# A windowed attention with a two-layer network on one core: the first batch's loads in two parts, shorter mask work on GpSimd, and a newly planned order

## The chip, the cores and the metric

The kernel runs on one core of one Trainium2 chip. The metric is the time of one execution in device microseconds (us). One profiled execution of the kernel before lies beside three timed runs of it.

## What is computed

The reference has two stages. A causal attention with a window of 64 runs over 8 batches, 8 heads, 576 tokens and a head dimension of 64; its result, laid out as 4608 tokens of 512 channels, goes through two matrix products with x * sigmoid(x) between them.

```python
scores = np.matmul(q, k.transpose(0, 1, 3, 2)) / np.sqrt(64)
mask = (rel >= 0) & (rel < 64)
attn = softmax(np.where(mask, scores, -1e9))
x = np.matmul(attn, v).transpose(0, 2, 1, 3).reshape(4608, 512)
h = x @ w_in                       # 512 x 2048
out = (h * (1.0 / (1.0 + np.exp(-h)))) @ w_out   # 2048 x 512
```

All five inputs lie in memory as 32-bit numbers; the loads turn them into 16-bit ones (bf16). The output is 32-bit.

## The kernel before

**Order.** Nothing is scheduled while the kernel is built. Every piece of work (a load, one transposition, the scores of some blocks, one product) is put into a list by `Plan.add` (L38), and `Plan.run` (L43) emits the pieces in the order of one long string, `ORDER` (L55): a word such as `93P2` says piece 93, on PE, into PSUM bank 2. Each engine then works through its own queue in that order, and waits where its next instruction lacks an operand or a free buffer. There are 1643 words. The costs and priorities given to `add` play no part at run time.

**Tiles.** The tokens are cut into 9 tiles of 512. Tile t needs the attention of 8 blocks of 64 tokens, for two "quads" of 4 heads each. One such piece of attention is a visit: scores on PE (L292), exponentials on ScalarE (`expo`, L307), a mask on VectorE (`masking`, L314), values on PE (L323), a reciprocal and a product on VectorE (L334, L338), and the transposition of the result into the tile's `xt` (`turn_out`, L442).

**Tile 0** is done plainly. Its attention comes in visits of four blocks, and the mask is added by four more matmuls per visit (L285, with `ident` and `block`). `first_plain` (L450) multiplies w_in with half a tile's 256 tokens, two feature tiles at a time and over four channel groups; quad 0 gives channel groups 0 and 1, quad 1 gives 2 and 3. For the first 256 tokens and the first four pairs the product is split in two pieces, so that the half with quad 0's channels can go first (`SPLIT` in the loop that makes the pieces). `silu_plain` (L461) writes the activations into `gall`, a ring of 10 slots for all tiles, and `second_plain` (L464) multiplies them with w_out.

**Tiles 1 to 8** go through a scheme with 7 products in place of 8: sums of tokens (`xsum`, L485 and L487) and of weights (`wsum1`, `wsum2`, L469) before the products (L507), copies ("forks", L523, on ScalarE or VectorE) and additions ("joins", L526, on VectorE) after them, the activation L529 into `gall`, sums of activations (`gsum`, L493 and L496), and the second layer's seven products (L519) with forks and joins again. The output of a tile is stored by SP (L533).

**Loads** are all issued by GpSimd (POOL) in the order of `ORDER`. Batch 0's and 1's q and k come as one transfer per quad and tensor (`load_quad`, L224: 128 partitions with 18 tokens each, 1152 numbers per partition), later batches head by head (L227). A quad's q or k is transposed by VectorE (`turn_quad`, L255 and L258, for batches 0 and 1; `turn_blocks`, L265 and L268, later) into `kT` and `qT`. The buffers `nat` alternate between even and odd batches, so a load waits until the batch two before it has been transposed. v is loaded in groups of 128 tokens (L235, with L233 and L239 to L241 for the rest) and copied to the other half of the partitions (L273, L275). Weights come in eight transfers each (L245, L248).

**Constants.** POOL fills `strip` and `ident` with ones and cuts each with two `affine_select` instructions (L184 to L187, L191 to L193). While the first loads are under way PE runs products of a zero tile ("fills", L895), 36 in all.

The names in the lists of instructions below: `nat_87` and `nat_86` are k and q of quad 0 for even batches, `nat_89` and `nat_88` those of quad 1; `nat_90` to `nat_93` serve the odd batches; `vv_98` and `vv_99` hold v of the even and odd batches.

## Time and profile before

| | us |
|---|---|
| median of 3 runs | 276.85 (275.15 to 277.24) |
| span of the profiled execution | 275.0 |
| PE, DVE, ACT, POOL busy in it | 264.7, 214.0, 195.6, 129.7 |
| last store landed, end of the span | 275.0 |

The page gives no other time for the profiled execution than its span, from the first to the last instruction. The median of the runs lies 1.8 above that span, so it holds some time around it or a slower execution. The clock that the throttle granted to PE was 1.000 over the whole span. The rows of the profile give a start and a duration in us, the engine, the line, the output and inputs with their shapes, and in brackets how long the engine had been idle and what ended that.

### The profile page before, as it was taken

The numbers are of one execution on the slowest core, as the hardware profiler recorded it, in microseconds if no ns is written. First come the engines' busy times: TensorE is split into PE (matmuls) and PEld (weight loads), VectorE is DVE, ScalarE is ACT, GpSimd is POOL, SyncE is SP. The second block draws the span as 40 slices with busy tenths as digits, with TensorE's granted clock in tenths as the row PEclk, the third lists the DMA queues.
The fourth block names the chain that finished last, engine by engine and source line by source line (L and its number), as shares of the span: only waits on it lengthen the run. The fifth ranks groups of instructions, "written<-read, shape, count | busy, mean of one in ns | idle before, by whom it ended". The sixth has DMA issues, their size and how long they took to land.

```text
span 275.0 us, 10018 instructions
## 1 busy us (share of the span) xinstructions
PE 264.7 (96%) x4335; PEld 218.0 (79%) x4342; DVE 214.0 (78%) x426; ACT 195.6 (71%) x361; POOL 129.7 (47%) x194
## 2 busy tenths in 40 slices
PE   7978999999999999999999999999999999999993
PEld 2557844688888888888888888888888888888882
DVE  3757578999996898889799999988867967824741
ACT  1555993699749993987499958893888489537910
POOL 7944566988959758596387335940000000000000
PEclk9999999999999999999999999999999999999999
DMA  6999999999999959999979998990400040003004
GB/s 106 167 190 210 198 191 172 144 198 157 118 151 209 127 56 97 242 122 87 93 179 159 83 126 122 136 121 2 155 0 2 6 155 0 2 29 127 0 2 157
DMA packets 101631, 31.62 MB, mean 115 GB/s; under 512 B 92368, under 2 KB 95440, under 8 KB 101584
## 3 DMA queue, kind: packets, MB, share of 16 engines
q0 software_dynamic: 96128, 21.51, 86.1%
q1 hardware_dynamic: 5456, 9.44, 9.7%
q8 instruction: 35, 0.57, 0.9%
q14 instruction: 12, 0.10, 0.1%
HBM read 42.99 MB, written 9.44 MB: 191 GB/s over the span
## 4 chain that ended last, share of the span: by engine, by line
PE 88%; ACT 4%; DVE 4%; issue 1%; ACTq 0%
PE room L519 36%; PE room L507 35%; PE room L292 4%; PE room L323 4%; PE room L450 4%; PE room L895 4%; PE room L464 2%; ACT es L307 2%; DVE o L338 1%; ACT L307 1%; ACT g L461 1%; DVE es L314 1%; DVE xt L442 1%; PE room L285 1%; ACT L461 0%
## 5 line engine op out<-in xcount | busy, mean ns | idle before, releaser
L529 ACT ACTIVATE g<-room 128x512 bf16<-128x512 f32 x96 | 53.6, 605 | 4.5 <-PE room L507 4.1
L507 PEld LDWEIGHTS <-wsum 128*128 128x128 bf16 x512 | 49.9, 98 | 7.2 <-issue 1.0
L519 PEld LDWEIGHTS <-gsum 128*128 128x128 bf16 x512 | 49.1, 98 | 6.2 <-DVE gsum L496 0.2
L507 PE MATMUL room<-xsum,wsum 128*128 128x256 bf16 x384 | 53.3, 272 | 0.5 <-ACT es L307 0.3
L307 ACT ACTIVATE es<-room 128x512 bf16<-128x512 f32 (+1 forms) x88 | 39.1, 533 | 14.2 <-PE room L292 9.6
L519 PE MATMUL room<-wsum,gsum 128*128 128x256 bf16 x384 | 48.4, 273 | 0.0
L507 PEld LDWEIGHTS <-w_in_sb 128*128 128x128 bf16 x384 | 37.2, 98 | 4.7
L519 PEld LDWEIGHTS <-g 128*128 128x128 bf16 x384 | 36.7, 98 | 4.6
L526 DVE TENSOR_TENSOR room<-room,part 128x512 f32<-128x512 f32 (+1 forms) x41 | 27.8, 684 | 13.7 <-ACT part L523 3.5
L227 POOL DMA_DIRECT2D nat<-in_k_dram x48 | 30.0, 631 | 15.1 <-DVE kT L265 11.4
L507 PE MATMUL room<-xt,w_in_sb 128*128 128x256 bf16 x256 | 36.8, 273 | 0.0
L519 PE MATMUL room<-w_out_sb,g 128*128 128x256 bf16 x256 | 35.7, 273 | 0.0
L227 POOL DMA_DIRECT2D nat<-in_q_dram x48 | 29.9, 637 | 9.7 <-DVE qT L268 6.1
L523 ACT COPY ot<-room 128x512 f32<-128x512 f32 (+1 forms) x23 | 13.3, 582 | 28.6 <-PE room L519 21.5
L235 POOL DMA_DIRECT2D vv<-in_v_dram x32 | 29.6, 940 | 5.0 <-DMA nat<-in_k_dram 1.7
L523 ACT COPY room<-room 128x512 f32<-128x512 f32 x40 | 23.3, 592 | 12.1 <-PE room L507 10.8
L526 DVE TENSOR_TENSOR fin<-room,part 128x512 f32<-128x512 f32 x32 | 21.6, 683 | 9.0 <-PE room L507 6.1
L523 ACT COPY part<-room 128x512 f32<-128x512 f32 x40 | 23.6, 598 | 6.4 <-PE room L519 3.2
L241 POOL DMA_DIRECT2D vv<-in_v_dram x24 | 22.3, 934 | 12.0 <-PE room L323 11.5
L314 DVE TENSOR_TENSOR es<-es,strip 128x1024 bf16<-128x1024 bf16 (+1 forms) x36 | 21.9, 626 | 6.7 <-ACT es L307 6.4
L338 DVE TENSOR_TENSOR o<-room,recips 128x896 bf16<-128x896 f32 (+2 forms) x36 | 25.9, 726 | 0.8
L496 DVE TENSOR_TENSOR gsum<-g,gsum 128x512 bf16<-128x512 bf16 x64 | 25.1, 415 | 0.4
(75 smaller groups left out, 376.8 us busy)
## 6 DMA issues: line engine op xcount, KB each, us to landing
out_dram<-ot SPq DMA_DIRECT2D x16, 512.0 KB, 3.9
vv<-in_v_dram POOLq DMA_DIRECT2D x56, 128.0 KB, 5.0
nat<-in_k_dram POOLq DMA_DIRECT2D x48, 72.0 KB, 4.0
nat<-in_q_dram POOLq DMA_DIRECT2D x48, 72.0 KB, 3.7
w_in_sb<-in_moe_w_in_dram POOLq DMA_DIRECT2D x8, 256.0 KB, 9.2
w_out_sb<-in_moe_w_out_dram POOLq DMA_DIRECT2D x8, 256.0 KB, 9.0
nat<-in_k_dram POOLq DMA_DIRECT2D x4, 288.0 KB, 8.0
nat<-in_q_dram POOLq DMA_DIRECT2D x4, 288.0 KB, 8.2
```

The costliest lines, as they stand in the source:

```text
L227: queue[e].dma_start(out=nats[b % 2][a][kk][32 * h:32 * h + 32].rearrange("p (n x) -> p n x", n=NB), in_=(q, k)[kk][b, 4 * a + h].rearrang ...
L235: queue[e].dma_start(out=vv[b % 2][:, :, 2 * g + 1, 0:D], in_=v[b, :, 128 * g:128 * g + 128].rearrange("h p d -> p h d"))
L241: queue[e].dma_start(out=vv[b % 2][:, :, 2 * g, 0:D], in_=v[b, :, 128 * g - 64:128 * g + 64].rearrange("h p d -> p h d"))
L307: nc.scalar.activation(out=es_part(a, blocks)[:, h], in_=banks[bank.idx][:, 0:64 * n], func=ACTF.Exp, scale=scale)
L314: nc.vector.tensor_mul(t, t, strip[:, s:s + n].rearrange("k n i -> k (n i)").unsqueeze(1).to_broadcast([128, 2, 64 * n]))
L338: nc.vector.tensor_mul(out, at_values(bank, n)[:, :, :, 0:D], recips[:, w:w + 2 * n].rearrange("k (t n) -> k t n", t=bank.wide).unsqueeze( ...
L496: nc.vector.tensor_sub(out=dst[2 * i - 1], in0=g(1, 2 - i), in1=dst[i - 1])
L507: nc.tensor.matmul(banks[bank.idx][:, 256 * i:256 * i + 256], lhsT=lhs(z, i), rhs=rhs(z), start=(start and i == 0 and z == 0), stop=(z == ...
L519: nc.tensor.matmul(banks[bank.idx][:, 256 * m:256 * m + 256], lhsT=lhs(m, i), rhs=rhs(i), start=(start and i == 0 and m == 0), stop=(stop ...
L523: copies[e](out=dst, in_=src)
L526: nc.vector.tensor_add(out=dst, in0=bank, in1=part)
L529: nc.scalar.activation(out=g_tile(pair, 256 * t, 256 * t + 256), in_=src.rearrange("k (f t) -> k f t", f=2), func=ACTF.Silu)
```

## The change

Seven edits go together.

1. q and k of batch 0 are loaded in two parts each, tokens 0 to 255 and 256 to 575 of a quad (128 KB and 160 KB as written, in place of 288 KB), and each part is transposed by an instruction of its own. There are eight loads and eight transpositions in place of four and four. `LOADS`, which makes the loads, lists first parts (`a`), two groups of v (`u`), second parts (`b`) and the other groups; the order of issue is that of `ORDER`.
2. POOL no longer fills `strip` and `ident`: VectorE does (`const_fills`), with zeros for `ident`, whose diagonal one `affine_select` with `not_equal` sets. POOL has three mask instructions in place of six.
3. Tile 0's activations go to `g_first`, a second view of `gsum`, in place of slots of `gall`. Tile 1's activations find the ring free; tile 1's activation sums must wait for tile 0's second layer.
4. All first-layer products of tile 0 are split by channel groups, not only the first four pairs of the first half. Tile 0's `xt` is laid out by halves (`by_half`).
5. The copies of the first two groups of batch 0's v may be made by ScalarE as well.
6. The last tile's stores may be issued by ScalarE's queue as well as by SP's.
7. `ORDER` is new throughout (1664 words). Of the 36 fills 15 stand ahead of the first scores, 24 before; the first scores are quad 1's. In the last tile ScalarE issues two of the five stores. Over the whole program VectorE makes 11 of the output copies in place of 5 (rows `COPY ot`), and ScalarE loads its function tables 16 times in place of 18.

```diff
 ORDER = (
-    "1D 9G 2D 74P7 3D 11G 69P2 72P5 13G 67P0 15G 68P1 73P6 5G 70P3 71P4 19G 7D 78P3 81P6 82P7 86P3 6G 10D 77P2 89P6 90P7 75P0 17G 76P1 80P5 12D 83P0 79P4 "
+    "1D 14G 5D 4D 2D 3D 83P4 16G 76P1 89P1 91P6 30G 110P7 80P5 93P4 10G 6G 28G 12G 82P1 96P1 15D 102P4 8D 7G 19G 17D 31D 18G 107P6 92P7 11D 95P6 105P1 "
...
-        nc.gpsimd.memset(strip[:, 0], 1.0)
...
     def const_ident(_):
-        nc.gpsimd.memset(ident, 1.0)
-        nc.gpsimd.affine_select(out=ident, in_=ident, compare_op=ALU.is_ge, fill=0.0, base=0, channel_multiplier=1, pattern=[[-1, 128]])
-        nc.gpsimd.affine_select(out=ident, in_=ident, compare_op=ALU.is_ge, fill=0.0, base=0, channel_multiplier=-1, pattern=[[1, 128]])
+        nc.gpsimd.affine_select(out=ident, in_=ident, compare_op=ALU.not_equal, fill=1.0, base=0, channel_multiplier=1, pattern=[[-1, 128]])
+
+    def const_fills(_):
+        nc.vector.memset(strip[:, 0], 1.0)
+        nc.vector.memset(ident, 0.0)
...
+    PARTS = ((0, 256), (256, 576))
+
+    def load_part(e, b, a, kk, i):
+        lo, hi = PARTS[i]
+        queue[e].dma_start(out=nats[b % 2][a][kk][:, 2 * lo:2 * hi], in_=(q, k)[kk][b, 4 * a:4 * a + 4, lo:hi].rearrange("h (p c) d -> h p (c d)", p=32))
...
+    def turn_part(b, a, kk, i):
+        lo, hi = PARTS[i]
+        c = (hi - lo) // 32
+        src = nats[b % 2][a][kk][:, 2 * lo:2 * hi].bitcast(FP32)
...
+            nc.vector.transpose(out=dst.rearrange("x (p c) -> x c p", c=c), in_=src.rearrange("x (c w) -> x c w", c=c))
...
+    g_first = gsum.rearrange("k u n f t -> k (u n f t)").rearrange("k (g f t) -> k g f t", g=8, f=2)
...
-            nc.scalar.activation(out=g_tile(pr, lo, hi), in_=src[:, i], func=ACTF.Silu)
+            nc.scalar.activation(out=g_first[:, pr, :, lo:hi], in_=src[:, i], func=ACTF.Silu)
...
-        nc.tensor.matmul(banks[bank.idx], lhsT=gall[:, pair, f % 2, 128 * m:128 * m + 128], rhs=w_out_sb[:, f],
+        nc.tensor.matmul(banks[bank.idx], lhsT=g_first[:, pair, f % 2, 128 * m:128 * m + 128], rhs=w_out_sb[:, f],
...
-    LOADS = "p0-2 u0-4 i0-2 i2-4 i4-6 r0-1 i6-8 o0-2 v0-1 o2-3 r1-2 o3-4 v1-2 u4-5 o4-5 v2-4 o5-8 v4-5"
+    LOADS = "a0-2 u0-2 b0-2 u2-4 i0-2 i2-4 i4-6 r0-1 i6-8 o0-2 v0-1 o2-3 r1-2 o3-4 v1-2 u4-5 o4-5 v2-4 o5-8 v4-5"
...
+                half = [x for nb in range(lo // 64, hi // 64) for x in xt_done[nb][:1]] + [win[ft // 2][0] for ft in fts]
...
-            st = p.add({"SP": 0.45}, lambda e, i=i, r0=r0, r1=r1, lo=lo, hi=hi: store(e, j, 2 * i + r0, 2 * i + r1, lo, hi), deps, 0,
+            st = p.add({"SP": 0.45, "ACT": 0.4} if last else {"SP": 0.45}, lambda e, i=i, r0=r0, r1=r1, lo=lo, hi=hi: store(e, j, 2 * i + r0, 2 * i + r1, lo, hi), deps, 0,
```

The new order is shown at three places. The first is the start of POOL's queue, which issues every load. Before:

```order
L224 DMA nat_87<-in_k_dram 128x1152
L224 DMA nat_86<-in_q_dram 128x1152
L224 DMA nat_89<-in_k_dram 128x1152
L224 DMA nat_88<-in_q_dram 128x1152
L184 MEMSET strip 128x64
L185 ISA
L185 AFFINE_SELECT strip<-strip 128x64
L187 AFFINE_SELECT strip<-strip 128x64
L235 DMA vv_98<-in_v_dram 128x8x64
L191 MEMSET ident 128x128
L192 AFFINE_SELECT ident<-ident 128x128
L193 AFFINE_SELECT ident<-ident 128x128
```

After:

```order
L233 DMA nat_89<-in_k_dram 128x1x512
L233 DMA nat_88<-in_q_dram 128x1x512
L233 DMA nat_88<-in_q_dram 128x1x640
L233 DMA nat_87<-in_k_dram 128x1x512
L185 ISA
L185 AFFINE_SELECT strip<-strip 128x64
L187 AFFINE_SELECT strip<-strip 128x64
L233 DMA nat_89<-in_k_dram 128x1x640
L233 DMA nat_86<-in_q_dram 128x1x512
L191 AFFINE_SELECT ident<-ident 128x128
L244 DMA vv_98<-in_v_dram 128x8x64 x2
L233 DMA nat_86<-in_q_dram 128x1x640
```

Eight part loads stand where four quad loads stood. The second parts are those of 640 numbers per partition. One of them comes ahead of the strip's masks and three behind, and two groups of v stand ahead of the last two (the last row here is the first of those).

VectorE's queue at the same place, where it transposes q and k of batch 0 (L255 and L258 before, L276 and L279 after). Before:

```order
L255 STREAM_TRANSPOSE kT_96<-nat_87 128x18x32
L258 STREAM_TRANSPOSE qT_94<-nat_86 128x9x64
L255 STREAM_TRANSPOSE kT_97<-nat_89 128x18x32
L258 STREAM_TRANSPOSE qT_95<-nat_88 128x9x64
L273 COPY vv_98<-vv_98 64x8x64
L205 MEMSET vv_99 128x72
L206 MEMSET vv_99 64x8x32
L275 COPY vv_98<-vv_98 64x8x64
```

After:

```order
L276 STREAM_TRANSPOSE kT_97<-nat_89 128x8x32
L199 TENSOR_SCALAR block<-strip 128x512
L200 MEMSET block 64x64
L279 STREAM_TRANSPOSE qT_95<-nat_88 128x4x2x32
L279 STREAM_TRANSPOSE qT_95<-nat_88 128x5x2x32
L276 STREAM_TRANSPOSE kT_96<-nat_87 128x8x32
L276 STREAM_TRANSPOSE kT_97<-nat_89 128x10x32
L279 STREAM_TRANSPOSE qT_94<-nat_86 128x4x2x32
L294 COPY vv_98<-vv_98 64x8x64
L296 COPY vv_98<-vv_98 64x8x64
L279 STREAM_TRANSPOSE qT_94<-nat_86 128x5x2x32
L276 STREAM_TRANSPOSE kT_96<-nat_87 128x10x32
```

The queue now begins with quad 1's k. First parts have 8 groups of 32 for k and 4 by 2 for q, second parts 10 and 5 by 2. The second parts of quad 0 (`nat_86`, `nat_87`) stand behind the first two copies of v.

The second place is VectorE's queue at the beginning of tile 1, from the sums of tokens (`xsum`) to the first joins (`room<-room,part`). Before:

```order
L485 TENSOR_TENSOR xsum<-xt_76 128x2x512
L487 TENSOR_TENSOR xsum<-xt_76,xsum 128x512
L469 TENSOR_TENSOR wsum_72<-w_out_sb 128x512 x2
L487 TENSOR_TENSOR xsum<-xt_76,xsum 128x512
L265 STREAM_TRANSPOSE kT_96<-nat_87 128x9x2x32
L526 TENSOR_TENSOR room<-room,part_79 128x512
L469 TENSOR_TENSOR wsum_72<-wsum_72,w_out_sb 128x512
L526 TENSOR_TENSOR room<-room,part_80 128x512
L526 TENSOR_TENSOR fin_81<-room,part_79 128x512
```

After:

```order
L511 TENSOR_TENSOR xsum<-xt_76 128x2x512
L513 TENSOR_TENSOR xsum<-xt_76,xsum 128x512 x2
L495 TENSOR_TENSOR wsum_72<-w_out_sb 128x512 x2
L495 TENSOR_TENSOR wsum_72<-wsum_72,w_out_sb 128x512
L495 TENSOR_TENSOR wsum_72<-w_out_sb 128x512
L495 TENSOR_TENSOR wsum_72<-wsum_72,w_out_sb 128x512 x2
L495 TENSOR_TENSOR wsum_72<-w_out_sb 128x512
L495 TENSOR_TENSOR wsum_72<-wsum_72,w_out_sb 128x512
L552 TENSOR_TENSOR room<-room,part_80 128x512
```

Eight rows of weight sums (`wsum_72`) now stand between the token sums and the first join; there were two and one transposition.

The third place is the end of batch 2's loads and their transposition, in the middle of tile 1. The last head of q of quad 1 is the last row with `nat_88` here. POOL before:

```order
L227 DMA nat_86<-in_q_dram 32x9x128
L227 DMA nat_88<-in_q_dram 32x9x128
L227 DMA nat_86<-in_q_dram 32x9x128
L239 DMA vv_98<-in_v_dram 64x8x64
L227 DMA nat_90<-in_q_dram 32x9x128
L227 DMA nat_88<-in_q_dram 32x9x128
L227 DMA nat_91<-in_k_dram 32x9x128
L227 DMA nat_90<-in_q_dram 32x9x128
L235 DMA vv_98<-in_v_dram 128x8x64
```

POOL after:

```order
L236 DMA nat_90<-in_q_dram 32x9x128
L250 DMA vv_98<-in_v_dram 128x8x64
L236 DMA nat_91<-in_k_dram 32x9x128
L242 DMA vv_99<-in_v_dram 64x8x64
L236 DMA nat_90<-in_q_dram 32x9x128 x2
L236 DMA nat_87<-in_k_dram 32x9x128
L236 DMA nat_88<-in_q_dram 32x9x128
L236 DMA nat_91<-in_k_dram 32x9x128
L244 DMA vv_98<-in_v_dram 128x8x64
L236 DMA nat_86<-in_q_dram 32x9x128
```

That load is row 55 of POOL's queue before and row 69 after; heads of batch 3 (`nat_90` to `nat_93`) and groups of v now stand ahead of it. VectorE's queue where that buffer is transposed into `qT_95`, before (the first row is a join) and after:

```order
L526 TENSOR_TENSOR fin_82<-room,part_80 128x512
L265 STREAM_TRANSPOSE kT_97<-nat_89 128x9x2x32
L268 STREAM_TRANSPOSE qT_94<-nat_86 128x9x2x32
L469 TENSOR_TENSOR wsum_72<-w_out_sb 128x512
L526 TENSOR_TENSOR room<-room,part_79 128x512
L268 STREAM_TRANSPOSE qT_95<-nat_88 128x9x2x32
L469 TENSOR_TENSOR wsum_72<-w_out_sb,wsum_72 128x512
L493 TENSOR_TENSOR gsum<-g 128x2x512
L526 TENSOR_TENSOR fin_81<-room,part_79 128x512
L526 TENSOR_TENSOR room<-room,part_80 128x512
```

```order
L519 TENSOR_TENSOR gsum<-g 128x2x512
L522 TENSOR_TENSOR gsum<-g,gsum 128x512
L495 TENSOR_TENSOR wsum_72<-w_out_sb,wsum_72 128x512
L289 STREAM_TRANSPOSE qT_95<-nat_88 128x9x2x32
L519 TENSOR_TENSOR gsum<-g 128x2x512
L286 STREAM_TRANSPOSE kT_96<-nat_91 128x9x2x32
L522 TENSOR_TENSOR gsum<-g,gsum 128x512 x2
L335 TENSOR_TENSOR es_84<-es_84,strip 128x1024
L552 TENSOR_TENSOR room<-room,part_79 128x512
L335 TENSOR_TENSOR es_84<-es_84,strip 128x1024
```

The transposition of `nat_88` stood in front of the first sum of activations (`gsum`); it now stands behind six such sums, and more of them and masks (`es`) follow it.

65 lines of the change are left out of this document (37 added, 28 removed), and 119 rows, old and new, of the table ORDER.

## Prediction

> **What bounds the kernel.** I read the page's head first, then the busy time by stretches, then the timelines of PE, VectorE and POOL over the first 23 us, the chain of waits, and last the end of the span. Rows of the stretches give start and end, the length, and the busy us and instructions of PE, of its weight loads, of VectorE, ScalarE and POOL.
>
> ```profile
> span 275.0 us, 10018 instructions
> ...
> 17.70:22.40 4.70, 3.74 (x69) 2.78 (x59) 3.81 (x10) 1.08 (x2) 2.28 (x4) 1.00 1.22 209
> 34.00:40.00 6.00, 5.81 (x56) 2.54 (x55) 4.78 (x11) 5.92 (x12) 3.50 (x6) 1.00 1.60 189
> 40.00:46.00 6.00, 5.52 (x118) 2.77 (x121) 4.83 (x13) 3.84 (x9) 3.66 (x7) 1.00 1.56 191
> 46.00:52.40 6.40, 6.08 (x119) 3.14 (x121) 5.76 (x17) 2.20 (x6) 5.66 (x10) 1.00 1.15 112
> 52.40:75.00 22.60, 22.60 (x320) 19.62 (x318) 22.50 (x46) 21.48 (x40) 20.84 (x32) 1.00 1.63 166
> 75.00:100.00 25.00, 24.73 (x513) 21.28 (x512) 21.48 (x43) 19.76 (x36) 17.08 (x26) 1.00 1.35 139
> ```
>
> PE is the bound from 22 us to the end: it leaves 0.96 us idle from 17.7 to 22.4, 0.99 in the three stretches from 34 to 52.4 (0.19, 0.48 and 0.32), none from 52.4 to 75, and 0.27 in the next 25. So little can be won behind 52.4 us, and a lot can be lost there: from 52.4 to 75 VectorE is full too (22.50 of 22.60). What can be won lies ahead of the first products.
>
> ```profile
> 1.39 7.60 PE L895 MATMUL room<-fill 128*128 128x512 bf16 x24 [1.39 <-DVE fill L213]
> 9.36 0.42 PE L292 MATMUL room<-qT,kT 32*128 32x64 bf16 x32
> 12.76 0.41 PE L292 MATMUL room<-qT,kT 32*128 32x64 bf16 x32
> ...
> 17.74 1.26 PE L450 MATMUL room<-xt,w_in_sb 128*128 128x256 bf16 x8
> 22.42 7.91 PE L450 MATMUL room<-xt,w_in_sb 128*128 128x256 bf16 x71 [0.51 <-DVE xt L442]
> 52.23 1.04 PE L507 MATMUL room<-xt,w_in_sb 128*128 128x256 bf16 x8
> ```
>
> The fills are no work of the program, so the real work starts at 9.36 with scores; the first product of w_in is at 17.74, and the products run without a break from 22.42. Tile 1 begins at 52.23.
>
> ```profile
> 5.58 1.25 DVE L255 STREAM_TRANSPOSE kT<-nat 128x576 f32<-128x576 f32 x1 [0.48 <-DMA nat<-in_k_dram]
> 7.06 1.21 DVE L258 STREAM_TRANSPOSE qT<-nat 128x576 f32<-128x576 f32 x1 [0.22 <-DMA nat<-in_q_dram]
> 8.48 1.26 DVE L255 STREAM_TRANSPOSE kT<-nat 128x576 f32<-128x576 f32 x1 [0.21 <-DMA nat<-in_k_dram]
> 9.89 1.23 DVE L258 STREAM_TRANSPOSE qT<-nat 128x576 f32<-128x576 f32 x1
> ...
> 15.50 0.70 POOL L245 DMA_DIRECT2D w_in_sb<-in_moe_w_in_dram  x1 [1.21 <-DMA w_in_sb<-in_moe_w_in_dram]
> 17.65 0.71 POOL L245 DMA_DIRECT2D w_in_sb<-in_moe_w_in_dram  x1 [1.45 <-DMA w_in_sb<-in_moe_w_in_dram]
> 18.94 0.54 POOL L248 DMA_DIRECT2D w_out_sb<-in_moe_w_out_dram  x1 [0.57 <-DMA w_in_sb<-in_moe_w_in_dram]
> ...
> w_in_sb<-in_moe_w_in_dram POOLq DMA_DIRECT2D x8, 256.0 KB, 9.2
> ```
>
> Three of VectorE's four transpositions start as their transfer lands, so transfers of 288 KB land 1.48, 1.42 and 1.41 us apart, 200 KB per us. POOL goes on each time a transfer of w_in has landed: 256 KB in 1.29 (17.65 to 18.94), 198 KB per us. The loads are one stream that runs at a rate. The first quad is ready to be scored at 7.06 + 1.21 = 8.3 and the second at 11.1.
>
> **The parts and the start.** The stream seems to begin at 5.58 - 1.43 = 4.15. In parts, at 200 KB per us, 128 KB take 0.64 and 160 KB 0.80. By the new queue: k of quad 1 lands at 4.8, q at 5.4, its second part at 6.2, k of quad 0 at 6.9, the second part of quad 1's k at 7.7, q of quad 0 at 8.3. A first transposition has 256 of 576 tokens and takes about 1.25 x 256/576 = 0.56 us. So the first scores can start at 6.0 in place of 8.3, and those of the other quad at 8.9 in place of 11.1. Ahead of them stand 15 fills. At the mean of the 24 (0.317 us) these end at 6.1; the first ones are the slower ones as PE starts up, so I take 7.0, and 0.5 for the added masks: first scores at 7.5 in place of 9.36.
>
> What comes behind the parts: from the last q (9.9) to the first w_in (15.4) the stream brought four groups of v and 256 KB, so a group of v takes (5.5 - 1.3) / 4 = 1.05. In the new queue the first w_in has all parts and three groups ahead of it: 8.3 + 1.6 + 3.2 + 1.3 = 14.4. The first product needs quad 0's four blocks: scores to 9.8, four exponentials, values, and VectorE's 1.4 us (below), as well as w_in. Before, 4.98 us lay between the second quad's scores (12.76) and the first product; with 8.9 to 9.8 for these scores it comes at 13.9 to 14.8, with the weights at 14.4, and PE's queue has other scores and values in between. I take 15.4, so 2.3 us earlier than 17.74.
>
> ```profile
> 15.54 0.21 DVE L334 RECIPROCAL recips<-room 128x8 f32<-128x8 f32 x1 [1.69 <-PE room L323]
> 16.54 0.45 DVE L442 STREAM_TRANSPOSE xt<-o 128x256 f32<-128x256 f32 x1
> 21.92 0.45 DVE L442 STREAM_TRANSPOSE xt<-o 128x256 f32<-128x256 f32 x1
> ```
>
> All of tile 0's products are now split by quad. That keeps PE busy while the last transposition (21.92, which PE waited 0.51 for) is outstanding; of the 0.96 us idle ahead of 22.42 I take 0.6. Together the start is worth -2.9 us; the bounds are -1.5 (the first scores' 1.9 less a group of work that has to wait) and -4.1 (the first product right at 14.5 and all 0.96).
>
> What rows of whole transfers can't show is a price for each transfer. A line through both sizes has 0.36 us at no bytes if 288 KB take 1.41, and none if they take 1.48; four transfers more cost 0 to 1.4 us by that. A group of v has 128 KB and took 1.05, which would make a part as slow and cost 2.7 for the eight; but v is written 128 bytes at a time, w_in 1024, and the parts 1024 and 1280, so w_in's rows are the nearest, and I take 0. The far end, that a part takes what a whole takes, is a rival. The Trainium skill, DMA: Bandwidth & Descriptors, in the section on the anatomy of one DMA on the SWDGE (gpsimd) path, gives 2.0 us for each DMA plus its bytes over 436 KB per us. One behind the other, eight parts would by that take 18.7 us and four wholes 10.7, and the sum would come out 8 us higher, near 281.6, an estimate from that page. The trace disagrees: wholes landed 1.42 apart, under the 2.0 alone.
>
> POOL issues four loads more and three mask instructions fewer:
>
> ```profile
> 2.14 0.55 POOL L224 DMA_DIRECT2D nat<-in_q_dram  x1
> 5.39 0.23 POOL L191 MEMSET ident<- 128x128 bf16 x1
> ```
>
> That is 4 x 0.55 - 3 x 0.23 = 1.5 us more in all. It costs nothing: from 15.50 on POOL waits for landings, so it is ahead of the stream. Without that cover it would be 1.5. VectorE's two fills take 0.1 to 0.2 at a time when it waits for loads; the masks of POOL wait for them, but stand behind four loads.
>
> **Tile 0's second layer** has no work more or less. Its activations in `gsum` ask that tile 1's first sums wait for the second layer's end, and these sums come some 10 us behind it (their rows stand below): nothing. The chain shows ScalarE between 31 and 37:
>
> ```profile
> 30.98 1.28 ACT L307
> ...
> 33.23 1.28 ACT L461
> ...
> 36.59 1.28 ACT L307
> ```
>
> Three function table loads of 1.28 stand in it. Two fewer in the program, and free slots of `gall`, give back at most the 0.99 us that PE idles from 34 to 52.4; I take -0.4. PE reaches tile 1 at 52.2 - 3.3 = 48.9.
>
> **Tile 1** has the tightest place.
>
> ```profile
> 53.46 0.75 DVE L469 TENSOR_TENSOR wsum<-w_out_sb 128x512 bf16<-128x512 bf16 x2
> 55.16 0.68 DVE L526 TENSOR_TENSOR room<-room,part 128x512 f32<-128x512 f32 x1
> 61.19 0.77 DVE L268 STREAM_TRANSPOSE qT<-nat 128x576 f32<-128x576 f32 x1
> 62.19 0.68 DVE L493 TENSOR_TENSOR gsum<-g 128x1024 bf16<-128x1024 bf16 x1
> 68.25 0.42 DVE L496 TENSOR_TENSOR gsum<-g,gsum 128x512 bf16<-128x512 bf16 x1
> ...
> 62.23 0.62 POOL L227 DMA_DIRECT2D nat<-in_k_dram  x1
> 65.07 1.80 POOL L227 DMA_DIRECT2D nat<-in_q_dram  x3
> ...
> nat<-in_q_dram POOLq DMA_DIRECT2D x48, 72.0 KB, 3.7
> ```
>
> Ahead of the first joins stand eight weight sums in place of two and a transposition (0.77): 6 x 0.37 - 0.77 = 1.4 us more. The join at 55.16 came 2.9 behind PE's first product, so most of it is taken from slack in PSUM banks, and the weight sums are missing further on. I take +0.3, between 0 and +1.1.
>
> The transposition of batch 2's last q is moved behind 16 more loads (4 by the parts, 12 others) and behind most of `gsum`. The load that it needs is now the 68th. The 68th of before is the first of the three issued at 65.07, and lands by the median of such loads near 69.4. By bytes the new 68th is the old 64th, issued 2.8 earlier (62.23): 66.6. POOL waits for VectorE there, which is 3 us ahead: 63.6. VectorE comes to it at 64 to 66 (68.67 less 3, and less rows that moved back). What waits behind it in VectorE's queue are sums and masks, and PE's second layer for them. I take +0.3, between 0 and +3.
>
> **The rest.** Visits that are moved or joined in pairs run the same matmuls; I count nothing. All other places of the new order from 75 us on are costed at nothing too: PE idles 0.27 of 25 there, so the gain is at most some tenths, and a loss of 0 to 3 (a gap of 0.3 in each of the last seven tiles, and one of 1) can't be excluded by any row.
>
> ```profile
> 270.40 0.37 ACT L523 COPY ot<-room 128x256 f32<-128x256 f32 x1 [2.65 <-PE room L519]
> L533 SPq DMA_DIRECT2D out_dram<-ot x5: 345/418/691, 267.8 to 271.5; - x5
> ```
>
> At the end the last copy is done at 270.8, and SP issues the last store at 271.5, since the one ahead took up to 0.69. With two of five on ScalarE's queue that is -0.5 (0 to -0.7).
>
> **Sum:** -2.9 - 0.4 + 0.3 + 0.3 - 0.5 = -3.2. The span goes from 275.0 to 271.8, and the median from 276.85 to 273.6. (It lies 1.8 over the span of the profiled execution, and I carry the difference over.)
>
> **Rivals.** *The lead is given back at tile 1.* If the 68th load lands as it did before, at 69.4, VectorE stands still from about 65 and reaches tile 2's masks no earlier than before. The lead of 3 is gone, the end's -0.5 remains, and the sums behind it come late by up to 1, say 0.3: 276.6. For it speaks VectorE at 22.50 of 22.60; against it, that POOL is held there by VectorE, which is ahead.
>
> *The weights bind.* The stream carries the same bytes, so the last transfers of w_out land no sooner:
>
> ```profile
> 43.59 0.60 POOL L227 DMA_DIRECT2D nat<-in_k_dram  x1 [0.43 <-DMA w_out_sb<-in_moe_w_out_dram]
> ```
>
> One of them is seen to land just ahead of 43.59. The second layer goes through its eight transfers in 18 us (from about 34 to 52.2), 2.3 each; starting at 31 it needs the seventh at 44.6, with 1 to spare if that is the one. If the new queue lets it land 2.6 later, 1.6 of the lead is lost: 275.2.
>
> *Parts as slow as wholes* (slower). At 1.42 for each of eight, the parts take 11.4 in place of 5.7. The first w_in lands at 20.1 and the first product comes 2.6 later than before; with the other terms that is +2.6 - 0.4 + 0.3 + 0.3 - 0.5 = +2.3, 279.1, and more if w_out binds as well. It decides from about 1.1 us per part. Against it speaks that 256 KB took less than 288; for it, that a group of v took 1.05 for 128 KB.
>
> **Chances.** The forecast 0.53 (own range 271.0 to 275.2), the lead given back 0.20, the weights 0.15, slow parts 0.12. 1% is 2.8 us, about what a measurement of this kernel can tell from no change: faster is under 274.1, slower over 279.6. Faster takes four fifths of the forecast and some of the second rival: 0.48. Slower takes the upper part of the last rival and of the open loss behind 75 us: 0.10. The same: 0.42. The range for 8 in 10 goes from 271.0, the forecast's lower end (all bounds of a gain at once: -4.1 - 0.99 - 0.7 = -5.8), to 277.4, the upper end of the first rival, and leaves the last out.
>
> **What would show it.** In the profile of the changed kernel: the eight transpositions of batch 0 starting 0.6 to 0.8 apart as they land (1.4 would be the slow parts); first scores at 7.5; the first product of w_in at 15.4, and no gap of PE's ahead of 22; tile 1's first product at 49; no wait of VectorE for a q load near 64; PE full from there to 267; ScalarE's queue among the last stores. The prediction is wrong if PE has gaps between 50 and 75, or small ones at many joins further on, where nothing of the profile before speaks for or against the new order.

## The result, and the profile after

The changed kernel takes 285.76 us (median of 4 runs, 285.29 to 286.55); the kernel before took 276.89 beside it (275.15 to 277.24). The ratio is 1.031, with a 95% interval of 1.026 to 1.036. The forecast was 273.6, with a range up to 277.4, so the result lies on the other side, 12.2 us away. The profiled execution has a span of 284.2 us (275.0 before) and itself took 285.87; PE's granted clock was 0.998 in it.

The head of its page, with the engines' busy time, and the shares of the chain that ended last:

```profile
span 284.2 us, 10017 instructions
...
PE 267.3 (94%) x4342; PEld 217.8 (77%) x4342; DVE 216.4 (76%) x438; ACT 191.4 (67%) x353; POOL 132.2 (47%) x195
...
PE 65%; DVE 11%; DMA 10%; POOL 6%; issue 4%; ACT 2%; DVEq 0%; POOLq 0%
```

The span grew by 9.2 us and PE's busy time (264.7 before) by 2.6: most of what grew is time in which PE stood. Of the chain before, PE had 88%, and no transfer was listed in it; now VectorE, transfers and POOL hold 27%.

The start, first on VectorE, for the eight transpositions of batch 0:

```profile
7.04 0.64 DVE L276 STREAM_TRANSPOSE kT<-nat 128x256 f32<-128x256 f32 x1 [4.26 <-DMA nat<-in_k_dram]
8.56 0.63 DVE L279 STREAM_TRANSPOSE qT<-nat 128x256 f32<-128x256 f32 x1 [0.58 <-DMA nat<-in_q_dram]
11.15 0.75 DVE L279 STREAM_TRANSPOSE qT<-nat 128x320 f32<-128x320 f32 x1 [1.96 <-DMA nat<-in_q_dram]
11.75 0.61 DVE L276 STREAM_TRANSPOSE kT<-nat 128x256 f32<-128x256 f32 x1
12.99 0.75 DVE L276 STREAM_TRANSPOSE kT<-nat 128x320 f32<-128x320 f32 x1 [0.64 <-DMA nat<-in_k_dram]
...
17.26 0.76 DVE L279 STREAM_TRANSPOSE qT<-nat 128x320 f32<-128x320 f32 x1 [0.61 <-DMA nat<-in_q_dram]
17.86 0.72 DVE L276 STREAM_TRANSPOSE kT<-nat 128x320 f32<-128x320 f32 x1
```

They were to start 0.6 to 0.8 apart, from 4.8 on. They start at 7.04 and up to 3.7 apart (from 13.58, not shown, to 17.26), each within 0.3 us of its part's landing. On PE the same stretch reads:

```profile
9.24 0.42 PE L313 MATMUL room<-qT,kT 32*128 32x64 bf16 x32 [0.61 <-DVE qT L279]
...
13.79 0.42 PE L313 MATMUL room<-qT,kT 32*128 32x64 bf16 x32 [2.50 <-DVE kT L276]
...
20.95 1.04 PE L474 MATMUL room<-xt,w_in_sb 128*128 128x256 bf16 x8
```

The first scores come at 9.24 (forecast 7.5, before 9.36), and the first product of w_in at 20.95 (forecast 15.4, before 17.74): 3.2 us later.

The rest by stretches, in the columns of the prediction (the third column is PE's busy time), of the changed kernel:

```profile
52.40:75.00 22.60, 22.57 (x250) 17.93 (x245) 22.12 (x48) 20.04 (x36) 19.05 (x30) 1.00 1.45 157
75.00:100.00 25.00, 24.79 (x513) 21.34 (x511) 21.95 (x42) 19.17 (x37) 18.66 (x27) 1.00 1.36 141
100.00:150.00 50.00, 48.78 (x860) 41.88 (x848) 42.68 (x82) 35.93 (x64) 34.15 (x50) 1.00 1.23 124
150.00:200.00 50.00, 47.09 (x941) 40.15 (x940) 42.42 (x83) 39.23 (x71) 26.62 (x34) 1.00 1.13 104
```

and of the kernel before, where the prediction had stopped looking:

```profile
100.00:150.00 50.00, 50.00 (x861) 43.63 (x859) 43.89 (x83) 38.08 (x69) 36.74 (x53) 1.00 1.34 137
150.00:200.00 50.00, 49.78 (x1031) 43.06 (x1029) 44.73 (x86) 38.97 (x70) 20.15 (x26) 1.00 1.03 106
```

PE idles 4.13 us of these hundred, 0.22 before. Followed by milestones, the last first-layer product of tile 0 starts 3.0 us later than before (37.04 against 34.01), half of tile 4's second layer is reached 4.3 later (160.92 against 156.65), that of tile 6 10.0 later, and the last product starts 9.25 later (279.34 against 270.09). Behind it the end takes 4.85, before 4.95.

So there are two losses, of 3.2 us at the start and of some 6 behind 75 us. To size the second one, the time from one matmul's start to the next, less the usual length for its shape, was summed over all places where it is 0.13 us or more, from 52 to 270 us: 1.61 us before, 7.44 after.

### The profile page after: what moved, and what is told of

It is laid out like the page before. It is cut to its first block, busy times and chain, and to the rows that moved or that the text cites. A ratio compares the mean times of both kernels' runs of the same rounds, so it can differ in the third digit from the quotient of the medians.

```text
span 284.2 us, 10017 instructions
## 1 busy us (share of the span) xinstructions
PE 267.3 (94%) x4342; PEld 217.8 (77%) x4342; DVE 216.4 (76%) x438; ACT 191.4 (67%) x353; POOL 132.2 (47%) x195
## 4 chain that ended last, share of the span: by engine, by line
PE 65%; DVE 11%; DMA 10%; POOL 6%; issue 4%; ACT 2%; DVEq 0%; POOLq 0%
PE room L545 27%; PE room L533 24%; PE room L474 5%; DMA nat<-in_q_dram 4%; PE room L490 4%; PE room L344 3%; DMA w_in_sb<-in_moe_w_in_dram 3%; PE room L313 3%; POOL nat L236 2%; DVE o L359 2%; DVE qT L289 2%; ACT es L328 2%; POOL vv L250 1%; DMA vv<-in_v_dram 1%; DVE es L335 1%
## 5 line engine op out<-in xcount | busy, mean ns | idle before, releaser
L545 PE MATMUL room<-wsum,gsum 128*128 128x256 bf16 x384 | 50.1, 273 | 1.0 <-DVE gsum L522 0.4
L545 PE MATMUL room<-w_out_sb,g 128*128 128x256 bf16 x256 | 35.1, 273 | 0.1
L359 DVE TENSOR_TENSOR o<-room,recips 128x896 bf16<-128x896 f32 (+2 forms) x36 | 25.2, 722 | 0.7
L549 ACT COPY ot<-room 128x512 f32<-128x512 f32 (+1 forms) x17 | 9.7, 578 | 23.1 <-PE room L545 12.6
## 6 DMA issues: line engine op xcount, KB each, us to landing
nat<-in_q_dram POOLq DMA_DIRECT2D x2, 288.0 KB, 10.3
```

The source lines that it names most:

```text
L359: nc.vector.tensor_mul(out, at_values(bank, n)[:, :, :, 0:D], recips[:, w:w + 2 * n].rearrange("k (t n) -> k t n", t=bank.wide).unsqueeze( ...
L545: nc.tensor.matmul(banks[bank.idx][:, 256 * m:256 * m + 256], lhsT=lhs(m, i), rhs=rhs(i), start=(start and i == 0 and m == 0), stop=(stop ...
L549: copies[e](out=dst, in_=src)
```

## The experiments

All are edits of the changed kernel or of the one before. The table gives how much later than in the kernel before PE reaches three points of each profiled execution, and the ratio of the times.

| run | made from | first product of w_in | half of tile 1's second layer | last product | ratio (95%) |
|---|---|---|---|---|---|
| the change | | +3.21 | +3.66 | +9.25 | 1.031 (1.026 to 1.036) |
| e1_spread | after | +0.12 | +0.38 | +6.37 | 1.025 (1.014 to 1.037) |
| e2_whole | after | +0.84 | +0.26 | +7.47 | 1.027 (1.018 to 1.035) |
| e3_before_parts | before | +5.00 | +4.92 | +4.93 | 1.015 (1.009 to 1.021) |
| e7_heads_outer | before | +7.52 | +7.44 | +7.47 | 1.024 (1.021 to 1.027) |
| e10_before_spread | before | -0.02 | -0.05 | -0.03 | 1.005 (1.002 to 1.008) |
| e5_turns_later | after | +4.13 | +3.71 | +8.98 | 1.040 (1.034 to 1.045) |
| e6_more_fills | after | +3.97 | +4.24 | +8.59 | 1.032 (1.028 to 1.036) |
| e9_all_three | after | +1.68 | +1.89 | +4.97 | 1.018 (1.014 to 1.022) |
| e8_shift_before | before | -0.72 | +0.66 | +0.70 | 1.002 (1.000 to 1.004) |
| e11_shift_half | before | -0.41 | +1.52 | +3.17 | 1.017 (1.014 to 1.021) |
| e12_shift_whole | before | +3.56 | +3.49 | +3.66 | 1.007 (1.004 to 1.010) |

The points come from one execution of each, the ratio from all its runs; the two can differ by a us or two, as in e11 and e12. In five of the profiles PE's granted clock was 0.50 for a stretch of the start: for 10.24 us from 10.92 on in e7, 6.83 from 12.24 on in e3, and 3.41 from 15.54, 15.28 and 14.08 on in e5, e6 and e12. In the others, the changed kernel's and e1's among them, it was 1.00 throughout the work. Part of what those five lose ahead of the first product can therefore be the clock. The line of e7's page, in 40 slices of its span:

```profile
PEclk9759999999999999999999999999999999999998
```

### Why the parts are late: e1, e2, e3, e7

The transfers of the changed kernel from 1 to 12 us, first the busy share of the DMA engines in 40 slices:

```profile
DMA  0000000911324636565896967999589999999999
...
DMA packets 3525, 0.92 MB, mean 84 GB/s; under 512 B 2763, under 2 KB 3525, under 8 KB 3525
...
nat<-in_q_dram POOLq DMA_DIRECT2D x2, 160.0 KB, 8.4
...
nat<-in_k_dram POOLq DMA_DIRECT2D x2, 128.0 KB, 6.8
```

The same of the kernel before:

```profile
DMA  0000006899798999998999999999999999999999
...
DMA packets 3967, 1.61 MB, mean 146 GB/s; under 512 B 3455, under 2 KB 3455, under 8 KB 3967
...
nat<-in_k_dram POOLq DMA_DIRECT2D x2, 288.0 KB, 5.0
```

With the parts under way the engines are not slow, they are idle: a first part of 128 KB takes 6.8 us from issue to landing where a whole quad of 288 KB took 5.0. The cut also changed the shape of the source. A whole quad is written as 128 rows of 18 tokens, `(h p) (c d)`; a part, which no longer lies at one stride over heads and rows, as 4 heads of 32 rows, `h p (c d)`. The Trainium skill, DMA: Bandwidth & Descriptors, in the section on why a DMA increments its semaphore by 16 and not by 1, says that the number of engines that carry a transfer is the largest up to 16 that divides the outermost dimension of both sides: 16 for 128 rows, and only 4 for 4 heads. The traces agree. While the first transfer of e7 (below) is alone, from 3.5 to 4.5 us, four packets with data are under way at a time in 81 of 100 moments taken, and eight or nine from 5.0 to 5.5, when the second has joined; in the kernel before it is 17 on average from 4.5 to 8.5, in the changed one 3 from 3.0 to 4.5.

`e1_spread` keeps two parts, but takes for each part its share of every row's 18 tokens, so that the source has 128 rows again. It puts batch 0's tokens in wrong places; the work is the same.

```diff
-        queue[e].dma_start(out=..., in_=(q, k)[kk][b, 4 * a:4 * a + 4, lo:hi].rearrange("h (p c) d -> h p (c d)", p=32))
+        rows = (q, k)[kk][b, 4 * a:4 * a + 4].rearrange("h (p c) d -> (h p) (c d)", c=18)
+        queue[e].dma_start(out=..., in_=rows[:, 2 * lo:2 * hi])
```

> The changed kernel, with one thing else: each part of batch 0's q and k takes 8 or 10 of every partition's 18 tokens, so that its rows form one dimension of 128 and not 4 heads by 32; bytes, number of transfers and order stay (the tokens of batch 0 come to wrong places). Theory A, the shape: with 4 heads as the outermost dimension a part is carried by few of the 16 DMA engines. Then the parts land 0.6 to 0.9 apart, the last near 11, the first product of w_in is at 15 to 16 in place of 20.95, and the time falls by 4 to 6, to about 280, if the loss between 130 and 215 us belongs to the new order, and to 273 to 276 if that loss follows from the late start. Theory B, a price for each transfer: nothing moves, 285 to 286.

`e2_whole` leaves the order and all else as changed, but loads a whole quad where the first part was loaded, and nothing at the second.

```diff
-        queue[e].dma_start(out=nats[b % 2][a][kk][:, 2 * lo:2 * hi], in_=...)
+        if i == 0:
+            load_quad(e, b, a, kk)
```

> The changed kernel with the parts undone alone: at the place of each first part the whole 288 KB of the quad are loaded, at that of the second part nothing; the eight transpositions and the whole order stay. Theory A (shape) and theory B (price for each transfer) both have the wholes land about 1.43 apart from 5.6 to 9.9, the first product at 16 to 18. If the loss from 130 to 215 us follows from the late start the time is 275 to 277; if it is the new order's own, 280 to 283.

`e3_before_parts` is the kernel before, in its own order, with each quad of batch 0 loaded in the two parts of the change and transposed in two steps (the transpositions, and the condition that keeps later batches as they are, are left out here).

```diff
-        queue[e].dma_start(out=nats[b % 2][a][kk], in_=...)
+        for lo, hi in ((0, 256), (256, 576)):
+            queue[e].dma_start(out=nats[b % 2][a][kk][:, 2 * lo:2 * hi], in_=(q, k)[kk][b, 4 * a:4 * a + 4, lo:hi].rearrange("h (p c) d -> h p (c d)", p=32))
```

> The kernel before, its order untouched, with batch 0's four quad loads each issued as two part loads and turned by two transpositions. By both theories the last part lands at 14 to 16 in place of 9.9 and the first product of w_in 3 to 5 us later than 17.74. If a late start drags later losses behind it, the time is 284 to 286; if it costs only itself, 279.5 to 282.

`e7_heads_outer` is the kernel before, with nothing cut: the four whole loads of 288 KB take every second head, so that 4 heads are outermost. Batch 0's quads then hold other heads, with the same work.

```diff
+        if b == 0:
+            queue[e].dma_start(out=nats[0][a][kk], in_=(q, k)[kk][0, a:8:2].rearrange("h (p c) d -> h p (c d)", c=18))
+            return
```

> The kernel before, its order and its four whole transfers of 288 KB kept, but each takes every second head in place of four neighbours, so that its source has 4 heads by 32 rows as two dimensions in place of 128 rows as one (batch 0's quads then hold other heads). Theory A, the shape: the transfers land 2 to 4 us apart in place of 1.43, the last at 13 to 20, and the time is 280 to 288. Rival, the slow parts come of their number or their size: landings as before, the last at 9.9, 276 to 278.

The transfers of `e1_spread` in the same 11 us:

```profile
DMA  0000004959999899999989999999999999989999
...
nat<-in_q_dram POOLq DMA_DIRECT2D x2, 160.0 KB, 5.4
...
nat<-in_k_dram POOLq DMA_DIRECT2D x2, 128.0 KB, 3.8
```

and of `e7_heads_outer` from 1 to 16 us:

```profile
DMA  0000090329324965997986999999999999999999
...
nat<-in_k_dram POOLq DMA_DIRECT2D x2, 288.0 KB, 10.3
```

With 128 rows outermost the engines fill up in e1, the last part lands at 14.71 in place of 17.77, and the first product comes 3.1 us earlier than in the changed kernel. With 4 heads outermost and nothing else changed (e7), 288 KB take 10.3 us in place of 5.0, and the kernel before loses 7.5 us, all of it ahead of the first product. Of these, 5.3 are the later landing of the last load (15.18 against 9.86); the other 2.2 come behind it, with PE's granted clock at 0.50 up to 21.16. (The theory had 2 to 4 us between the four landings; they are 2.4, 0.4 and 1.2 apart.) The packets count it too. Over the whole program e1's kernel has 64 packets under 512 bytes more than the one before (92432 against 92368) for its four more transfers, 16 each; e7's has 1536 more for four transfers, 384 each; and the changed kernel has 3136 more, which is 64 + 8 x 384. So the shape, not the number of parts, costs the 3.2 us; between the changed kernel and e1, both at a clock of 1.00, it is worth 3.1.

Two things in these runs went against what I had thought, and the times of e1 and e2 miss their ranges by them: e1 took 284.70 us in place of about 280 or less, e2 284.29 in place of 283 or less, while e3 (281.58) and e7 (283.77) lie in theirs. Even with the shape mended, parts bring nothing: e1's first product is 0.12 us later than before, not 2.3 earlier, and with whole loads (e2) it is 0.84 later, behind a stop of PE of 0.71 that e1 doesn't have (such stops are looked at below). And e1 and e2 still end 6.4 and 7.5 us late, though they are level with the kernel before up to tile 1, while e3 and e7, in the old order, carry their late start to the end without adding to it.

### Whose is the loss behind 75 us: e10

`e10_before_spread` has the loads of e1 in the order of before: the edit of e3 with e1's shape.

> The kernel before with its own order, batch 0's quads loaded in two parts each and turned in two steps, the parts spread over all 128 rows of the source as in the kernel with spread parts (so batch 0's tokens stand in wrong places, with the same work). Theory (the loss behind 50 us belongs to the new order, not to the loads or the number of steps): the first product of w_in starts 0 to 1.5 us later than before, that shift stays constant to the end, 276.5 to 278.5 us. Rival (the added loads and transpositions themselves bring the loss): it grows by 5 us or more between 60 and 200 us, 282 to 285 us.

It took 278.25 us (276.74 to 280.06), 1.6 more than the kernel before beside it (276.63), while its profiled span is 275.1 and its milestones agree with before within 0.2 us from the first product to the last. What makes those 0.5% is thus not to be seen in its one profile, which is of the fastest of its twelve runs. Its five runs with a granted clock under 0.995 took 278.42 to 280.06 us, the seven others 276.74 to 278.56; whether the clock is the cause was not tested. Its stretches from 100 to 200:

```profile
100.00:150.00 50.00, 50.00 (x861) 43.66 (x859) 43.68 (x82) 38.09 (x69) 36.77 (x53) 1.00 1.34 137
150.00:200.00 50.00, 49.78 (x1030) 43.07 (x1029) 45.00 (x87) 38.98 (x70) 20.20 (x26) 1.00 1.02 107
```

PE is as full as before. With the same evenly carried parts the new kernel (e1) loses 6.4 us there and the old one none. Between these two stand the order of the pieces and the change's smaller edits (masks, the place of the activations, the split products, ScalarE's copies and stores), and no longer the loads.

### Which places: e5, e6, e9

Two kinds of gap stand out in the changed kernel's trace. The first, on VectorE's timeline:

```profile
99.86 0.78 DVE L289 STREAM_TRANSPOSE qT<-nat 128x576 f32<-128x576 f32 x1 [0.45 <-issue]
...
121.08 0.78 DVE L286 STREAM_TRANSPOSE kT<-nat 128x576 f32<-128x576 f32 x1 [0.89 <-DMA nat<-in_k_dram]
```

and on PE's just behind:

```profile
101.94 1.27 PE L545 MATMUL room<-wsum,gsum 128*128 128x256 bf16 x10 [0.36 <-DVE gsum L519]
...
122.50 0.60 PE L533 MATMUL room<-xsum,w_in_sb 128*128 128x256 bf16 x4 [0.42 <-DVE room L552]
```

VectorE waits for a load of q or k that has just landed, the sums and joins queued behind the transposition are late, and PE waits for them. The chain of waits shows where the load comes from:

```profile
115.48 0.78 DVE qT L289
116.26 0.28 issue
116.54 0.59 POOL nat L236
117.14 3.75 DMA nat<-in_k_dram
...
121.08 0.06 DVE kT L286
121.14 0.64 issue
121.78 0.62 DVE room L552
```

POOL, whose queue is in order, stood before a load into the buffer that the transposition at 115.48 frees; the load behind it is on its way for 3.75 us, and VectorE's next transposition is planned right there. In the kernel before, all but one of the transpositions past 52 us start 2.4 us or more after their load has landed; the new order has them at 0.08 (99.86), 0.19 (121.08) and 0.13 (160.49). The second kind:

```profile
168.60 0.64 PE L313 MATMUL room<-qT,kT 32*128 32x64 bf16 x59
170.97 0.23 PE L313 MATMUL room<-qT,kT 32*128 32x64 bf16 x5 [1.73 <-issue]
```

PE stops in the middle of 64 equal matmuls whose operands are all there.

`e5_turns_later` takes the changed kernel and moves four transpositions back in VectorE's order, and with them the loads that need their buffers. Of `ORDER` only the words at the places left and taken are shown. (It has 1610 words, and 1589 in the kernel before; 1664 and 1643 are the numbers of pieces, of which 54 fills are never emitted.)

```diff
-1657D 739D 650A
+673D 739D 1072G 691P
-784D 744D 821P0
+814D 744D 1075G 835D
-764D 749D 826D0
+829D 749D 1079G 751G
-1083D 1078D 1007D
+1057D 1078D 1023A
```

> The changed kernel with four of VectorE's transpositions of later batches' q and k (those that start 0.1 to 0.6 us after their load has landed, at 99.9, 121.1, 122.9 and 160.5 us) moved 3 to 7 rows back in VectorE's queue, ahead of the scores that need them, with the loads that wait for them; nothing else. Theory C, late loads that hold up the rows behind the transpositions: the four gaps of PE of 0.5 to 0.6 us at 101.3, 121.8, 161.3 and 163.1 go, and the time falls by 1.8 to 2.5, to 283.3 to 284. Rival, the order is tight there anyway: the gaps go to the next wait and the time falls by under 0.7.

`e6_more_fills` takes the changed kernel and adds 66 narrow fills to those at the start. They do nothing but move all later instructions of PE by 132.

```diff
+        if 10 <= len(warmed) <= 20:
+            for _ in range(6):
+                nc.tensor.matmul(banks[op_bank.idx][:, 0:16], lhsT=fill[:, 0:128], rhs=fill[:, 0:16], start=True, stop=True)
```

> The changed kernel with 66 more narrow fill products (16 columns) at 5 to 11 us, where PE waits for loads anyway: 132 more PE instructions ahead of everything. Theory D, the 1.91 us gap at 169 us, inside one group of 64 scores that has no operand to wait for, is PE running out of fetched instructions: with the instruction stream moved by 132 it goes, or shrinks under 0.5, and may come up at another dense group; the time falls by 1 to 2 if it doesn't come up again. Rival, a wait that the profile doesn't show: the gap stays in the same group at 1.5 to 2.

In e5 the gaps at 101.3, 121.8 and 161.25 are gone, but others of 0.79, 0.35 and 0.48 stand at 125.65, 134 and 161.5, and the stop inside the scores grew; the last product is only 0.27 us earlier than in the changed kernel, and the time is no better (287.36 us, where the theory had 283.3 to 284). So the late loads are real and yet not the one cause: VectorE's work there is due so closely that a step moved back is missing at the next join. In e6 the stop is gone:

```profile
169.44 0.68 PE L313 MATMUL room<-qT,kT 32*128 32x64 bf16 x64
```

All 64 run through. A new stop, of 1.35, stands after the 735th pair of a weight load and a matmul, near 50 us. e6 gains 2.3 us against the changed kernel between 162 and 170 us, after it had lost 1.2 up to there by larger gaps at the late loads; the last product is 0.7 earlier, and the time (285.41 us) the same within its interval.

`e9_all_three` has e2, e5 and e6 together.

> The changed kernel with three edits at once: whole quad loads, the three late transpositions placed later, and the 66 narrow fillers that move TensorE's instruction borders. Theory (the loss behind 50 us is a sum of separate places): the start gives 2 us back, the transposition places 1.1, the stop at 169 us 1.9, of which places next in line take back about half: 281 to 283 us. Rival (the new order is tight throughout, so that whatever is repaired shows up as a wait elsewhere): 284 to 285.5 us, as each edit alone.

It took 282.01 us (280.59 to 282.79), ratio 1.018: the middle of what the sum of places gave (281 to 283). The start is 1.5 us better than in the changed kernel, the gaps from 52 to 270 come to 4.81 us in place of 7.44, and the last product starts 4.3 us earlier. What stays, 4.81 us in fifteen places of 0.15 to 0.8 us, 3.2 more than before, was not taken apart further.

### PE's stops without a cause: e8, e11, e12

The kernel before has such a stop too, in the values of batch 0:

```profile
14.96 0.67 PE L323 MATMUL room<-vv,es 128*32 128x65 bf16 x44
17.21 0.60 PE L323 MATMUL room<-vv,es 128*32 128x65 bf16 x52 [1.58 <-issue]
```

Each matmul has a weight load of its own, and the records of these are complete. Counted by them from the start, the stop of before comes after the 224th pair, and that of the changed kernel at 169 us after the 2783rd: 128 + 96 and 21 x 128 + 95. In e1, e2 and e5 the stop also comes after the 2783rd, in e2 and e9 one after the 224th, and in e6 and e9 one after the 735th (5 x 128 + 95). The page of the changed kernel names a queue for instructions:

```profile
q8 instruction: 35, 0.57, 0.8%
```

35 packets of 16 KB go with 4342 such pairs, one for about 124, so stops that lie whole multiples of 128 pairs apart fit a block of instructions that arrives late. Three kernels shift the count in the kernel before by cutting early fills into nine narrow ones of the same total width: eight fills (e8, the 12th to 19th, as shown), four (e11, the 12th to 15th) and sixteen (e12, the 8th to 23rd). That moves what follows by 64, 32 and 128 pairs.

```diff
-        nc.tensor.matmul(banks[op_bank.idx][:, 0:FILL], lhsT=fill[:, 0:128], rhs=fill[:, 0:FILL], start=True, stop=True)
+        width = 57 if 12 <= len(warmed) <= 19 else FILL
+        for _ in range(9 if width == 57 else 1):
+            nc.tensor.matmul(banks[op_bank.idx][:, 0:width], lhsT=fill[:, 0:128], rhs=fill[:, 0:width], start=True, stop=True)
```

> The kernel before, with eight of TensorE's early fillers each cut into nine narrow ones of the same total width, so that TensorE has 128 more instructions ahead of batch 0's scores and the same time in them. Theory (the stop of 1.6 us at 15.4 us in the kernel before comes when TensorE's instructions have to be fetched at a block border inside a group of tiny matmuls, so its place hangs on the count of instructions alone): the stop moves out of that group, the first product of w_in starts at 17.0 to 17.5 us instead of 17.7, and because the weights then bind for a part, the time falls by only 0.2 to 0.8 us (276.1 to 276.7). Rival (the stop is a wait for VectorE's copies or for v that the trace puts under issue): the stop stays at 1.4 to 1.8 us and the time is unchanged (276.6 to 277.2).

> The kernel before with four early fillers each cut into nine narrow ones: TensorE's instructions move by 64 instead of 128. Theory (a stop comes only where a block border of 256 instructions falls deep inside a group of tiny matmuls): the first border now falls 13 matmuls behind four wide fillers and the second into wide products, so neither the stop at 15.4 us nor the one at 18.2 us of the kernel shifted by 128 appears; first product of w_in at 17.0 us, the last product 0.4 to 0.9 us earlier, 275.9 to 276.6 us. Rival (the values wait at this place anyway, for v or the weights): the stop or its time stays within 0.3 us, 276.6 to 277.4 us.

> The kernel before with sixteen early fillers each cut into nine narrow ones: TensorE's instructions move by 256, one whole block, so that a border falls where it fell before. Theory (block borders): the stop of 1.4 to 1.8 us is back near 15.5 us at the same matmul of batch 0's values, 276.6 to 277.4 us. Rival (any more instructions ahead of the group, or a slightly other time of the fillers, move it away): no stop over 0.6 us there.

The stop in `e8_shift_before`, then in `e11_shift_half`, then in `e12_shift_whole`:

```profile
19.76 0.41 PE L323 MATMUL room<-vv,es 128*32 128x65 bf16 x29 [1.35 <-issue]
```

```profile
21.28 0.93 PE L450 MATMUL room<-xt,w_in_sb 128*128 128x256 bf16 x7 [1.90 <-issue]
```

```profile
13.28 0.18 PE L292 MATMUL room<-qT,kT 32*128 32x64 bf16 x1 [1.72 <-issue]
```

In e8 the old stop goes, the first product comes at 17.02 as forecast, and a new stop stands after the 352nd pair (2 x 128 + 96), in the next values; the 0.7 us are lost again, and the time is the same (277.48, ratio 1.000 to 1.004). So the place hangs on the count: that half of the theory holds in all ten kernels that stop. The count alone does not make a stop, though: e3, e7 and e10 count as the kernel before does and have none over 0.5 us at any border. The sizes I could not forecast. e11 was to avoid both stops; it has one of 1.90 after the 352nd pair among wide products, where I had expected none, and another of 1.22 at 136.99, after the 2271st (17 x 128 + 95), and took 281.18. e12 was to bring the old stop back in the values; its stop of 1.72 comes after the 224th pair as before, but that is now in the scores, and at the 352nd, where the values are, stands only 0.3. It took 278.90; the time of its theory was 276.6 to 277.4.

The times of the queue's packets, which the traces hold, tell why one border costs 2 us and the next nothing. In all thirteen kernels one packet of 16 KB goes with each border, in order: the first with the 224th pair, the next with the 352nd, and so on, 430 in all. No pair behind a border starts earlier than 1.27 us after its packet's end, and all fourteen stops over 0.5 us end 1.31 to 1.72 us after it. In the kernel before the packet is under way from 14.86 to 15.82, while PE runs through narrow products, and the stop ends at 17.21; in e8 it is 17.32 to 18.21 for the 352nd pair, and 19.76. In e12 the packet for the 352nd ends at 18.47, PE gets there at 19.68, and hardly waits. So PE waits for the block, for as long as it is at the border too early; what sets the moment at which a packet starts stays open. Open as well is what else the three kernels lose: e8 took 0.9, e12 2.2 and e11 4.5 us more than the kernel before beside it. No version was found that beats the kernel before.

## Why the prediction was wrong

**The price for each transfer, taken at 0: the first step that failed.** The term for the start was -2.9 and measured +3.2. I chose the row for the parts by the bytes in a run (1024 and 1280, "w_in's rows are the nearest") and did not look at the order of the dimensions, which the diff shows in plain sight. e7 shows that the shape alone does it, and e1 that it is worth 3.1 us here. (The Trainium skill's rule on engines, DMA: Bandwidth & Descriptors, the section cited above, is the one that the prediction should have weighed; the traces agree with it by the four packets at a time and the 3.1 us.) The rival of slow parts had the sign and a time near it for the start (+2.6), but as a price for each part that does not depend on size, and not as what it was.

**The gain of the parts as such was not there either.** In e1 six parts have landed at 9.74 where I had 8.3, three groups of v and the other two parts at 15.56 (forecast 13.1), and the first w_in at 16.84 (14.4). In e10, where all eight follow one another, the last lands at 11.30 and the last whole quad of before at 9.86: 1.44 more for four more transfers, 0.36 each, the very upper end of "0 to 1.4 us" that the line through two sizes had given. I had the bound and took the other end. That the first product of e10 is level with before hides a price: before had its stop of 1.58 ahead of it, e10 has none, and e8, without that stop either, is 0.70 earlier (17.02 against 17.72). The end of the stream, not its beginning, sets the first product. It starts 3.2 us behind the landing of the last part both in the changed kernel (17.77 and 20.95) and in e1 (14.71 and 17.86): the last transpositions stand in VectorE's queue ahead of the reciprocals and of the transposition into `xt` that the product needs, while w_in, by which the prediction had set it, has landed 0.6 and 1.0 us before.

**"All other places of the new order from 75 us on are costed at nothing": the second failed step, and the larger one.** The open loss was bounded at 0 to 3; it is 5.8 us of gaps. I had compared the rows' order only near tile 1 and took PE's fullness in the old order as a sign that the new one would hold too. e10 beside e1 shows that the loss comes with the new order and the edits that go with it, not with the loads; e5, e6 and e9 show it as a sum: about 1.7 us right behind transpositions that are planned as their load lands, 1.9 in one stop of PE, and the rest in small waits for sums, masks and joins.

**The other terms.** The late transposition of batch 2's last q (+0.3) and the tight place of tile 1 (+0.3): the load lands at 71.14, and VectorE comes to the transposition at 72.06 and does not wait.

```profile
72.06 0.77 DVE L289 STREAM_TRANSPOSE qT<-nat 128x576 f32<-128x576 f32 x1
```

Both moments were forecast some 7 us earlier (63.6, and 64 to 66), of which the late start explains 5.5. Half of tile 1's second layer lies +3.66 where the start already had +3.2, so the two terms together are 0.45 in place of 0.6; that it is these two was not tested.

The table loads and `gall`'s slots (-0.4): PE idled 0.99 us from 34 to 52.4 before; in the same work, 3 us later, it idles 1.10 from 37.0 to 55.4. The gain is not there.

```profile
37.00:43.00 6.00, 5.33 (x85) 2.57 (x83) 4.09 (x8) 3.93 (x8) 3.43 (x5) 1.00 1.67 184
43.00:49.00 6.00, 6.00 (x161) 2.90 (x149) 4.87 (x16) 5.21 (x15) 4.38 (x7) 1.00 1.51 191
49.00:55.40 6.40, 5.97 (x90) 3.01 (x89) 6.02 (x16) 1.68 (x4) 5.65 (x10) 1.00 1.54 136
```

The stores (-0.5) brought 0.1: ScalarE does issue two of them, the last at 280.05, 0.7 after the last product begins, but the time from there to the landing is as before.

```profile
280.05 0.35 ACTq L559 DMA_DIRECT2D out_dram<-ot  x1
```

By its own list of signs the prediction fails from the first line: transpositions up to 3.7 apart, first product at 20.95, and small gaps at many joins further on. It holds for two: no wait of VectorE near 64, and ScalarE's queue among the last stores.

## What to carry to other kernels

When a load is cut, write down the outermost dimension of its source before and after: a cut that leaves 4 rows outermost in place of 128 leaves most of the DMA engines idle until several such loads are under way, whatever the bytes in a run. When the whole order of a full engine is planned anew, what it lost nowhere before it can lose everywhere, so the margin of each load to its first user has to be looked at through the whole program, and a plan that sets a transposition right at its load's landing will wait. And 1 us won or lost in a program like this can be the place of an instruction block's border, so a gain or loss of that size wants a second kernel that shifts PE's instructions and nothing else.

## What the runs showed of the hardware

- Four loads of 288 KB with 4 heads outermost land at 11.15 to 15.18 us and those with 128 rows at 5.56 to 9.86, from the same queue, and each brings 384 packets under 512 bytes more. While one of them is alone, four packets with data are under way at a time, and in the kernel before 17.
- A queue of evenly carried transfers has a price for each: 0.36 us, between parts of 128 and 160 KB and wholes of 288 KB (e10 against before).
- PE stops without a missing operand, for 0.5 to 2.7 us, after 128 n + 95 or 96 pairs of a weight load and a matmul: the 224th, 352nd, 735th, 2271st and 2783rd. Shifting the count moves the stop to other work. One packet of 16 KB on the instruction queue goes with each such border, and every stop over 0.5 us ends 1.31 to 1.72 us after its packet; what sets the packet's start was not settled.
- The granted clock of PE fell to 0.50 early in five profiles, for 3.41 to 10.24 us; in e7 this began at 10.92 us, while PE stood for 6.34 us up to 14.84. Fills that start 0.22 us apart at 1.00 started 0.42 apart under it.
